# A fused retention and two-layer network: first layer of one group plain, weight sums a group later, seven products from the first group on

## The chip, the cores and the metric

The kernel runs on one core of a Trainium2 chip. The core has five engines with a queue each: TensorE (PE in the profile, its weight loads PEld), VectorE (DVE), ScalarE (ACT), GpSimd (POOL) and SyncE (SP), which here issues the data transfers. An instruction that must wait holds up everything behind it in its own queue. The metric is the device time of one execution in microseconds (us), the median of several runs.

## The reference, cut to what matters

Retention over a sequence, and then a network of two layers on its output `x` (3072 tokens by 512):

```python
state = gamma * state + k_t (outer) v_t          # per batch and head, 64 x 64
y_t   = (1 / sqrt(64)) * q_t @ state
x     = y as (batch * sequence, heads * 64)      # 3072 x 512

h   = x @ w_in                                   # w_in 512 x 2048
g   = h * erf(softplus(h))
out = g @ w_out                                  # w_out 2048 x 512
```

There are 4 batches of 768 positions and 8 heads. All is fp32. The two products with `w_in` and `w_out` are most of the arithmetic.

## The kernel before, in words

Retention is worked off in 24 chunks of 128 tokens, numbered j. The network takes the first 512 tokens in groups 0 to 3 (a group is 512 columns of the first layer), all plainly. The 2560 others are taken 256 tokens at a time, in two groups per 256 tokens: groups 4 to 23. G0 is 4. `s`, the parity of g - G0, says which half of `w_in` and of `w_out` a group uses.

**First layer of a later group.** `hidden_steps` (L951) does not multiply plainly: 26 products of blocks (128 tokens, 128 rows, 256 columns) take the place of 32. They need sums of blocks of `w_in`, formed once per half (`W_SUMS`, 30 entries, `sum_in` at L340), and sums of blocks of `x`, formed once per 256 tokens (`X_SUMS`, 18 entries, `x_sums` at L930). The products go in turn to four PSUM banks ("hp" and "r"). ScalarE copies the first product that belongs to a block of h (L974, L976), and VectorE adds or subtracts each further one (L972), 18 per group. A product can't enter a bank before the earlier one has been read, so VectorE's place in its queue decides when TensorE goes on.

**Gate.** `gate_softplus` and `gate_erf` (ScalarE) and `gated` (VectorE, L854) make g in the tile E of the group.

**Second layer of a later group.** `project_part` (L1027) computes seven products in place of eight, for which `g_sums` (L1009) forms four sums S1 to S4 of E on VectorE and `last_steps` (`sums`, L354) forms four sums T1 to T4 of `w_out` for each half, once. T3 overwrites a block of `w_out`, so that the plain way is open only before it. `put_part` combines the outcome. Before the change the first two later groups, 4 and 5, do it plainly: `project_plain` (L1048), eight parts of four matmul instructions, and `put_plain`. The parts of group g - 1 stand between the steps of group g's first layer, after steps 14, 18 and 24, and after it.

**The order of the work** is written out by hand: the loop over g at the end of the kernel says after which step what is issued, on every engine. In the dictionary `order`, `next_chunk` are five VectorE operations that prepare the next attention chunk, `e_sums` are the S sums, and `last_steps` are the T sums. `sub_begin`, `sub_states` and `sub_visit` are the attention of one chunk, of which `sub_visit(j, g)` stands after the first layer.

**Around group 4.** The 30 sums of `w_in`, half 0, are formed before or in group 4: 16 while the weights are still converted from 64 bits, 4 before the loop, the last 10 between its first ten steps. Those of half 1 follow: 20 on GpSimd (L344) and 10 on VectorE after the layer. The second layer of group 3, 32 matmul instructions of 512 columns (`project`, L901), stands in four parts before, in and after group 4's first layer; then `put_first` copies its four PSUM tiles (L916) and sends them out.

In matmul counts: TensorE does an fp32 matmul as two instructions in the profile, each with its own weight load.

Of the kernel before, what the change touches and what calls it, by code (L numbers as in the profile page):

```python
# [12 lines left out]
F32 = mybir.dt.float32  # L13
# [6 lines left out]
P = 128  # L20
C = 128
TCH = 512
# [114 lines left out]
def kernel(  # L137
# [202 lines left out]
    def sum_in(s, upto, engine=None):  # L340

        assert all(("hidden", 2 * FG + s * FG + u) in done for u in range(FG))
        for to, a, b, sign in W_SUMS[in_sums[s] : upto]:
            (engine or nc.vector).tensor_tensor(  # L344
                w_in_sb[:, s, to], w_in_sb[:, s, a], w_in_sb[:, s, b], op=OP[sign]
            )
        in_sums[s] = max(in_sums[s], upto)
# [12 lines left out]
    def weights():  # L360


        pending = [conversion(n) for n in range(n_p)]
        begun = 0
        for n, steps in enumerate(pending):
            for k, _ in enumerate(steps, start=begun):
                yield
                if n > 4 and n + 1 < n_p and k == 2:
                    next(pending[n + 1])
                    yield  # L370
            begun = int(n > 4)
            if pieces[n] == ("out", 5):
                for k in range(4, 17, 4):
                    sum_in(0, k)
                    yield

    def later_sums():
        for s in range(2):
# [334 lines left out]
    def sub_begin(j, pool=None):  # L713
        SC[j] = [ret_psum(pool) for _ in range(2)]
        sub_scores(j)
        sub_additions(j)

    def sub_visit(j, g):
# [44 lines left out]
        if c:  # L763
            of_state(0)
        last = chunk_of(g - 1)
        if (g - G0) % 2 == 1 and g > G0 + 1:
            clear.update((("o", 0), ("o", 1)))
        new = [
            None if g == G0 else O[last][3][:, 1, :].rearrange("p (u d) -> p u d", d=D),
# [47 lines left out]
    def gate_softplus(g):  # L817


        name = "r" if g < G0 + 2 and g % 2 else "e"  # L820
        E[g] = act.tile([P, N], F32, name=name, bufs=1)
        nc.scalar.activation(E[g], HS[g], AF.Softplus)  # L822

# [85 lines left out]
            done.add(("project", g))  # L909
        pace_around(3.4)  # L910

    def put_first():
        r = act.tile([P, N], F32, name="r", bufs=1)
        for tt in range(TT):
            o = r[:, tt * d_model : (tt + 1) * d_model]
            nc.scalar.copy(o, O[0][tt])  # L916
            nc.sync.dma_start(out[tt * P : (tt + 1) * P, :], o)

    G0 = n_ft // FG
    NG = G0 + (B * S - TCH) // SCH * 2
# [4 lines left out]
    def chunk_of(g):  # L927
        return TCH // SCH + (g - G0) // 2
# [22 lines left out]
    def hidden_steps(g):  # L951

        m, s = chunk_of(g), (g - G0) % 2
        HS[g] = act.tile([P, N], F32, name="h")
        banks = [pool.tile([P, FG, P], F32, name=name) for pool, name in ((ps_h, "hp"), (ps_r, "r")) for _ in range(2)]
        written = set()
        for w, x, bank, first, reads in STEPS:
            to = banks[bank]
            for u in range(2):
                nc.tensor.matmul(  # L960
                    to[:, u, :],
                    w_in_sb[:, s, w, u * P : (u + 1) * P],
                    XS[m](x),
                    start=first and u == 0,
                    stop=True,
                    skip_group_check=True,
                )
            of = to[:, :2].rearrange("p u t -> p (u t)")
            for o, plus in reads:
                h = h_block(g, o)  # L970
                if o in written:
                    nc.vector.tensor_tensor(h, h, of, op=ALU.add if plus else ALU.subtract)  # L972
                elif plus:
                    nc.scalar.copy(h, of)  # L974
                else:
                    nc.scalar.activation(h, of, AF.Copy, scale=-1.0)  # L976
                written.add(o)
            yield

    G = {}  # L980

# [55 lines left out]

    started = set()
    R = {}

    def project_plain(g, i):
        m, s = chunk_of(g), (g - G0) % 2
        t, fh, pair = i // 4, i % 4 // 2, i % 2
        if m not in O:
            O[m] = {i: ps_o.tile([P, 2, DH], F32, name=f"o{i}") for i in (0, 1, 3)}
        for u in range(2 * pair, 2 * pair + 2):
            at = (2 * fh + t) * TCH + u * P
            nc.tensor.matmul(  # L1048
                O[m][t],
                E[g][:, at : at + P],  # L1050
                w_out_sb[:, s, 2 * fh : 2 * fh + 2, u, :],
                start=(s == 0 and i % 4 == 0 and u == 0),
                stop=(s == 1 and i % 4 == 3 and u == 3),
                skip_group_check=True,
            )

    def put_plain(m, t):
        if t == 0:
            R[m] = act.tile([P, 8, DH], F32, name="r", bufs=1)
        r = R[m][:, 2 * t : 2 * t + 2].rearrange("p a c -> p (a c)")  # L1060
        nc.scalar.copy(r, O[m][t].rearrange("p a c -> p (a c)"))
        nc.sync.dma_start(out[m * SCH + t * P : m * SCH + (t + 1) * P, :], r)

    def put_part(m, step):

# [127 lines left out]
    def all_of(steps):  # L1193
        for _ in steps:
            pass

    all_of(weight_steps)

    idle = const.tile([P, 2], F32, name="idle_scalar")
    nc.gpsimd.memset(idle, 1.0)  # L1200

    j = JPC + 2
    gated(G0 - 1)
    all_of(prepared(j))
    load(JPC + 4)
    project(G0 - 1, 0)
    x_sums(G0)
    sub_begin(j)
    sub_states(j)
    sum_in(0, 20)  # L1210

    plain, put = (G0, G0 + 1), None
    for g in range(G0, NG):
        first, even = g == G0, (g - G0) % 2 == 0
        more = j < NJ
        if put is not None and put > chunk_of(G0):
            put_part(put, 0)
        e_sums = iter(()) if g - 1 in plain or first else g_sums(g - 1)
        next(e_sums, None)
        next_chunk = prepared(j + 1) if even or put is None else iter(())  # L1220

        if put is not None:
            order = {18: (e_sums,), 20: (e_sums,), 24: (e_sums, e_sums)}
        else:
            order = {
                10: (next_chunk,), 14: (next_chunk, e_sums), 16: (next_chunk, e_sums),
                18: (next_chunk, e_sums), 20: (e_sums,), 24: (next_chunk,),
            }
        if first:
            order = {n: (next_chunk,) for n in (12, 16, 18, 20, 22)}  # L1230
        elif g == G0 + 2:
            order.update({n: (last_steps,) for n in (12, 15, 20, 22)})
        elif g == G0 + 3:
            order.update({n: (last_steps,) for n in (14, 16)})
        elif g == G0 + 4:
            order.update({n: (last_steps,) for n in (12, 22)})
        for n, _ in enumerate(hidden_steps(g), start=1):
            if first:
                sum_in(0, min(20 + n, len(W_SUMS)))
                if n == 10:  # L1240
                    project(g - 1, 1)
                    nc.gpsimd.tensor_copy(idle[:, :1], w_in_sb[:, 0, W_SUMS[-1][0], :1])
                    sum_in(1, 20, nc.gpsimd)
            if put is not None and n in (14, 16, 18):
                if put > chunk_of(G0):
                    put_part(put, n // 2 - 6)
                elif n < 18:
                    put_plain(put, n // 2 - 7)
            for steps in order.get(n, ()):
                next(steps, None)  # L1250
            if not first and n in (14, 18, 24):
                part = (14, 18, 24).index(n)
                if g - 1 in plain:
                    project_plain(g - 1, part)
                else:
                    project_part(g - 1, (1, 2, 4)[part])
        put = None
        all_of(e_sums)
        all_of(next_chunk)

        nc.scalar.activation(idle[:, 1:], idle[:, 1:], AF.Softplus)
        gate_softplus(g)
        if more:
            sub_visit(j, g)
        if g + 1 < NG and not even:
            x_sums(g + 1)
        if more:
            if even and not first:
                all_of(prepared(j + 2))
            if j + 3 < NJ:  # L1270
                load(j + 3)
            j += 1
        gate_erf(g)
        if first:
            sum_in(1, len(W_SUMS))
            for tt in range(2, TT):
                project(g - 1, tt)
            put_first()
        else:
            if g - 1 in plain:  # L1280
                for part in range(3, 8):
                    project_plain(g - 1, part)
            else:
                for p in (5, 6, 7, 3):
                    project_part(g - 1, p)
            if even:
                put = chunk_of(g - 1)
        if g == NG - 1:
            last_gated(g)
        else:  # L1290
            gated(g)
# [59 lines left out]
```

## Time and profile before

The median is 672.5 us (three runs, 672.39 to 672.66). The profiled execution has a span of 670.3 us.

| engine | busy us | share of the span | instructions |
|---|---|---|---|
| TensorE, matmul | 658.7 | 98% | 6192 |
| TensorE, weight loads | 547.4 | 82% | 6192 |
| VectorE | 510.6 | 76% | 1095 |
| ScalarE | 272.8 | 41% | 395 |
| GpSimd | 22.1 | 3% | 42 |

| operation | instructions | mean ns of one |
|---|---|---|
| first layer, product of 128 columns (L960) | 2080 | 275 |
| second layer, seven products, 256 columns (L1027) | 1000 | 379 to 382 |
| second layer, plain, 512 columns (L1048) | 64 | 596 |
| VectorE, product into h (L972) | 360 | 416 to 419 |
| VectorE, sum of `w_out` blocks (L354) | 8 | 1218 |
| VectorE, S sum (L1009) | 68 | 677 to 685 |
| VectorE, sum of `w_in` blocks (L344) | 40 | 427 |
| GpSimd, sum of `w_in` blocks (L344) | 20 | 782 |

How to read it: matmuls overlap in the array, so the mean duration of one is longer than the time from one start to the next, and a busy TensorE is not one at its peak. Where an engine's idle time is given with a releaser ("<-DVE h L972"), that is the instruction whose end let it go on.

### The profile page before, as it was taken

To read this page: it belongs to the slowest core of one execution; us is meant where nothing else is said; L and a number is where in the kernel's file an instruction comes from. 1 tells how busy PE (TensorE), PEld (TensorE's weight loads), DVE (VectorE), ACT (ScalarE), POOL (GpSimd) and SP (SyncE) were. 2 spreads that over 40 slices of the span, in tenths; PEclk is the share of its full clock that TensorE was granted. 3 is DMA by queue.
4 is the path that set the end of the run, shared out by engine and by line. 5 is a ranking of instruction groups with operands and counts; after the bars stand their busy time and mean duration, and the time that the engine had idled before them with its cause. 6 is when DMAs were issued, how large, how long until landed. Compare 5 with 4: busy or idle time off the path is not lost.

```text
span 670.3 us, 15241 instructions
## 1 busy us (share of the span) xinstructions
PE 658.7 (98%) x6192; PEld 547.4 (82%) x6192; DVE 510.6 (76%) x1095; ACT 272.8 (41%) x395; POOL 22.1 (3%) x42
## 2 busy tenths in 40 slices
PE   8999999989999999999999999999999999999998
PEld 7744444466766998999999999999999999999997
DVE  5999999986778679678678787787687688476464
ACT  3467453425333344243343442442542542533440
POOL 1000000253000000000000000000000000000000
PEclk9999999999999999999999999999999999999999
DMA  9999744333321222322222221231232220000000
GB/s 188 227 253 240 196 138 97 62 61 62 105 45 29 68 42 45 69 45 47 60 51 46 47 65 36 46 80 35 45 78 38 42 55 1 2 32 1 1 33 31
DMA packets 156725, 47.68 MB, mean 71 GB/s; under 512 B 143088, under 2 KB 147568, under 8 KB 156656
## 3 DMA queue, kind: packets, MB, share of 16 engines
q1 hardware_dynamic: 156240, 46.72, 31.8%
q8 instruction: 48, 0.79, 0.5%
q14 instruction: 21, 0.17, 0.1%
q10 hardware_dynamic: 416, 0.01, 0.0%
HBM read 40.39 MB, written 6.29 MB: 70 GB/s over the span
## 4 chain that ended last, share of the span: by engine, by line
PE 77%; DVE 9%; SPq 5%; issue 3%; DMA 3%; ACT 2%; DVEq 0%; ACTq 0%
PE o L1027 33%; PE hp L960 22%; PE r L960 11%; SPq L187 4%; PE o L1048 4%; DMA kq<-in_k_dram 2%; PE r L741 2%; PE hp L633 1%; DVE w_out_sb L317 1%; PE o L901 1%; DVE w_out_sb L325 1%; PE o L777 1%; DVE xs L325 1%; DVE h L972 1%; DVE w_in_sb L331 1%
## 5 line engine op out<-in xcount | busy, mean ns | idle before, releaser
L960 PE MATMUL hp<-xs,w_in_sb 128*128 128x128 f32 x1040 | 146.3, 276 | 4.7 <-DVE h L972 3.8
L960 PEld LDWEIGHTS hp<-xs,w_in_sb 128*128 128x128 f32 x1040 | 134.6, 192 | 12.3 <-DVE h L972 7.2
L972 DVE TENSOR_TENSOR h<-h,hp 128x256 f32<-128x256 f32 x200 | 81.9, 419 | 77.9 <-PE hp L960 73.4
L1027 PE MATMUL o<-w_out_sb,h 128*128 128x256 f32 (+1 forms) x584 | 129.5, 379 | 0.4 <-DVE r L1306 0.4
L1027 PEld LDWEIGHTS o<-w_out_sb,h 128*128 128x128 f32 x584 | 108.6, 190 | 15.4 <-DVE r L1306 0.6
L1027 PE MATMUL o<-w_out_sb,e 128*128 128x256 f32 x432 | 102.2, 379 | 0.0
L822 ACT ACTIVATE e<-h 128x2048 f32<-128x2048 f32 x21 | 40.1, 1911 | 123.0 <-DVE h L972 123.0
L1027 PEld LDWEIGHTS o<-w_out_sb,e 128*128 128x128 f32 x432 | 78.2, 191 | 8.5
L972 DVE TENSOR_TENSOR h<-h,r 128x256 f32<-128x256 f32 x160 | 60.1, 416 | 25.1 <-PE r L960 23.7
L974 ACT COPY h<-hp 128x256 f32<-128x256 f32 x40 | 14.9, 373 | 153.1 <-PE hp L960 124.9
L960 PE MATMUL r<-xs,w_in_sb 128*128 128x128 f32 x480 | 66.7, 275 | 0.8 <-DVE am L640 0.8
L960 PEld LDWEIGHTS r<-xs,w_in_sb 128*128 128x128 f32 x480 | 60.1, 192 | 1.4 <-PE hp L960 0.9
L865 PE MATMUL hp<-xT,w_in_sb 128*128 128x512 f32 (+2 forms) x144 | 56.5, 548 | 0.0
L854 DVE TENSOR_TENSOR e<-h,e 128x1024 f32<-128x1024 f32 x40 | 46.9, 1214 | 8.1 <-ACT e L835 8.1
L960 PE MATMUL hp<-xT,w_in_sb 128*128 128x128 f32 x320 | 48.9, 275 | 0.0
L865 PEld LDWEIGHTS hp<-xT,w_in_sb 128*128 128x128 f32 x144 | 25.8, 190 | 27.0 <-issue 24.6
L960 PEld LDWEIGHTS hp<-xT,w_in_sb 128*128 128x128 f32 x320 | 43.6, 192 | 2.3 <-issue 1.4
L835 ACT ACTIVATE e<-e 128x2048 f32<-128x2048 f32 (+1 forms) x22 | 40.2, 1833 | 0.2
L976 ACT ACTIVATE h<-hp 128x256 f32<-128x256 f32 x60 | 23.0, 384 | 32.1 <-PE hp L960 30.7
L960 PE MATMUL r<-xT,w_in_sb 128*128 128x128 f32 x240 | 33.3, 275 | 0.0
L835 ACT ACT_TABLE_LOAD x24 | 30.8, 1283 | 0.4
L960 PEld LDWEIGHTS r<-xT,w_in_sb 128*128 128x128 f32 x240 | 30.0, 192 | 0.0
(161 smaller groups left out, 811.6 us busy)
## 6 DMA issues: line engine op xcount, KB each, us to landing
w_out_sb<-in_moe_w_out_dram SPq DMA_DIRECT2D x14, 512.0 KB, 5.6
kq<-in_k_dram SPq DMA_DIRECT2D x23, 256.0 KB, 4.0
v<-in_v_dram SPq DMA_DIRECT2D x23, 256.0 KB, 3.2
out_dram<-r SPq DMA_DIRECT2D x23, 256.0 KB, 2.7
kq<-in_q_dram SPq DMA_DIRECT2D x288, 16.0 KB, 1.8
kb<-in_k_dram SPq DMA_DIRECT2D x288, 16.0 KB, 1.7
w_in_sb<-in_moe_w_in_dram SPq DMA_DIRECT2D x8, 512.0 KB, 11.1
w_in_sb<-in_moe_w_in_dram SPq DMA_DIRECT2D x8, 256.0 KB, 8.8
```

Of the source, the lines that this page charges most:

```text
L187: nc.sync.dma_start(to[part, u * C : (u + 1) * C].rearrange("p (a d) -> p a d", d=32), src[2 * u + s, :, d * 32 : (d + 1) * 32].rearrange( ...
L325: nc.vector.scalar_tensor_tensor(power, hi, 1 << 31, power, op0=ALU.bitwise_and, op1=ALU.bitwise_or)
L822: nc.scalar.activation(E[g], HS[g], AF.Softplus)
L835: nc.scalar.activation(E[g][:, half], E[g][:, half], AF.Erf)
L854: nc.vector.tensor_tensor(E[g][:, half], HS[g][:, half], E[g][:, half], op=ALU.mult)
L865: nc.tensor.matmul(HP_[ft][:, t], w_in_of(ft, kk), XC[0][:, kk, t], start=(kk == 0), stop=(kk == n_k - 1),)
L960: nc.tensor.matmul(to[:, u, :], w_in_sb[:, s, w, u * P : (u + 1) * P], XS[m](x), start=first and u == 0, stop=True, skip_group_check=True,)
L972: nc.vector.tensor_tensor(h, h, of, op=ALU.add if plus else ALU.subtract)
L974: nc.scalar.copy(h, of)
L976: nc.scalar.activation(h, of, AF.Copy, scale=-1.0)
L1027: nc.tensor.matmul(O[m][i][:, half, at], G[g][a][:, u * P : (u + 1) * P], w_out_sb[:, s, OUT[b], u, at], start=i not in started, stop=(s = ...
L1048: nc.tensor.matmul(O[m][t], E[g][:, at : at + P], w_out_sb[:, s, 2 * fh : 2 * fh + 2, u, :], start=(s == 0 and i % 4 == 0 and u == 0), sto ...
```

## The change: what it does and what it is for

Group 4's first layer is computed plainly, by the new `hidden_plain`: eight tiles of four matmuls with 256 columns, each copied by ScalarE. It needs no sums of `w_in`. So the sums of half 0 move from ahead of group 4 to after it (10 on VectorE, 20 on GpSimd), where group 6 is the first to need them, and those of half 1 go all to VectorE, during and after group 4's first layer. The second layer of groups 4 and 5 is done with seven products as that of all others is: `project_plain` and `put_plain` go, the T sums of half 0 move to group 5 and those of half 1 to group 6, and the S sums of groups 4 and 5 are added. The second layer of group 3 stands behind group 4's first layer as a whole, and `put_first` sends each of its tiles out as soon as it is done, by way of the places in group 3's gate tile that the tile's matmuls have read. The aim is to let TensorE start group 4 without waiting for sums, and to spare an eighth of two groups' second layer.

```diff
-            if pieces[n] == ("out", 5):
-                for k in range(4, 17, 4):
-                    sum_in(0, k)
-                    yield
...
-        name = "r" if g < G0 + 2 and g % 2 else "e"
+        name = "r" if g < 4 and g % 2 else "e"
...
+    def put_first(tt):
+        o = E[G0 - 1].rearrange("p (u t c) -> p t u c", u=FG, t=TT)[:, tt]
+        nc.scalar.copy(o, O[0][tt].rearrange("p (u c) -> p u c", u=FG))
...
+    def hidden_plain(g):
...
+        for f, u in itertools.product(range(2), range(FG)):
+            to = ps_h.tile([P, TCH], F32, name="hp")[:, :SCH]
+            for kk in range(n_k):
+                nc.tensor.matmul(
+                    to, w_in_of((2 * f + s) * FG + u, kk), x[:, kk], start=kk == 0, stop=kk == n_k - 1
+                )
+            nc.scalar.copy(h[:, f, u], to.rearrange("p (t c) -> p t c", t=2))
+            yield
...
-    load(JPC + 4)
-    project(G0 - 1, 0)
-    x_sums(G0)
-    sub_begin(j)
-    sub_states(j)
-    sum_in(0, 20)
+    load(j + 2)
+    for n, _ in enumerate(hidden_plain(G0), start=1):
+        if n == 3:
+            sub_begin(j)
+    x_sums(G0)
+    sub_states(j)
+    all_of(prepared(j + 1))
+    sum_in(1, 20)
+    project(G0 - 1, 0)
+    nc.scalar.activation(idle, idle, AF.Softplus)
+    gate_softplus(G0)
+    sub_visit(j, G0)
+    load(j + 3)
+    put_first(0)
+    gate_erf(G0)
+    sum_in(1, len(W_SUMS))
+    for tt in range(1, TT):
+        project(G0 - 1, tt)
+        put_first(tt)
+    gated(G0)
+    sum_in(0, 10)
+    sum_in(0, len(W_SUMS), nc.gpsimd)
...
+        if g <= G0 + 2:
+            order = {
+                10: (next_chunk,), 12: (last_steps,), 14: (next_chunk, e_sums), 16: (last_steps,),
+                18: (next_chunk, e_sums), 20: (last_steps,), 22: (next_chunk,), 24: (next_chunk, e_sums),
+            }
...
+        if g <= G0 + 2:
+            next(last_steps)
...
-            if g - 1 in plain:
-                for part in range(3, 8):
-                    project_plain(g - 1, part)
-            else:
-                for p in (5, 6, 7, 3):
-                    project_part(g - 1, p)
+        for p in (5, 6, 7, 3):
+            project_part(g - 1, p)
```

More of the change, by code (lines that the diff above doesn't have):

```diff
@@ L765, in sub_visit @@
         last = chunk_of(g - 1)
-        if (g - G0) % 2 == 1 and g > G0 + 1:
+        if (g - G0) % 2 == 1:
             clear.update((("o", 0), ("o", 1)))
@@ L910, in project @@
         pace_around(3.4)
[L912 to L917, printed above, removed]
+    def put_first(tt):
+        o = E[G0 - 1].rearrange("p (u t c) -> p t u c", u=FG, t=TT)[:, tt]
+        nc.scalar.copy(o, O[0][tt].rearrange("p (u c) -> p u c", u=FG))
+        nc.sync.dma_start(out[tt * P : (tt + 1) * P, :].rearrange("p (u c) -> p u c", u=FG), o)
     G0 = n_ft // FG
@@ L978, in hidden_steps @@
             yield
+    def hidden_plain(g):
+        m, s = chunk_of(g), (g - G0) % 2
+        HS[g] = act.tile([P, N], F32, name="h")
+        h = HS[g].rearrange("p (f t u c) -> p f u t c", f=2, t=2, u=FG)
+        x = XC[m // 2][:, :, m % 2 * SCH : (m % 2 + 1) * SCH]
+        for f, u in itertools.product(range(2), range(FG)):
[6 more added lines that the diff above has]
+            yield
+        done.update(("hidden", (2 * f + s) * FG + u) for f in range(2) for u in range(FG))
     G = {}
@@ L1039 @@
     R = {}
[L1041 to L1062, printed above, removed]
     def put_part(m, step):
@@ L1197 @@
     all_of(weight_steps)
-    idle = const.tile([P, 2], F32, name="idle_scalar")
+    idle = const.tile([P, 1], F32, name="idle_scalar")
     nc.gpsimd.memset(idle, 1.0)
@@ L1204 @@
     all_of(prepared(j))
-    load(JPC + 4)
-    project(G0 - 1, 0)
-    x_sums(G0)
-    sub_begin(j)
-    sub_states(j)
-    sum_in(0, 20)
-    plain, put = (G0, G0 + 1), None
-    for g in range(G0, NG):
-        first, even = g == G0, (g - G0) % 2 == 0
+    load(j + 2)
[6 more added lines that the diff above has]
+    sum_in(1, 20)
+    project(G0 - 1, 0)
+    nc.scalar.activation(idle, idle, AF.Softplus)
[11 more added lines that the diff above has]
+    sum_in(0, len(W_SUMS), nc.gpsimd)
+    j += 1
+    put = None
+    for g in range(G0 + 1, NG):
+        even = (g - G0) % 2 == 0
         more = j < NJ
-        if put is not None and put > chunk_of(G0):
+        if put is not None:
             put_part(put, 0)
-        e_sums = iter(()) if g - 1 in plain or first else g_sums(g - 1)
-        next(e_sums, None)
+        e_sums = g_sums(g - 1)
+        next(e_sums)
         next_chunk = prepared(j + 1) if even or put is None else iter(())
@@ L1228 @@
             }
[L1229 to L1236, printed above, removed]
-        for n, _ in enumerate(hidden_steps(g), start=1):
[L1238 to L1243, printed above, removed]
+        if g <= G0 + 2:
[3 more added lines that the diff above has]
+            }
+        for n, _ in enumerate(hidden_steps(g), start=1):
             if put is not None and n in (14, 16, 18):
[L1245 to L1248, printed above, removed]
+                put_part(put, n // 2 - 6)
             for steps in order.get(n, ()):
                 next(steps, None)
-            if not first and n in (14, 18, 24):
-                part = (14, 18, 24).index(n)
-                if g - 1 in plain:
-                    project_plain(g - 1, part)
-                else:
-                    project_part(g - 1, (1, 2, 4)[part])
+            if n in (14, 18, 24):
+                project_part(g - 1, {14: 1, 18: 2, 24: 4}[n])
         put = None
@@ L1259 @@
         all_of(next_chunk)
-        nc.scalar.activation(idle[:, 1:], idle[:, 1:], AF.Softplus)
+        nc.scalar.activation(idle, idle, AF.Softplus)
         gate_softplus(g)
@@ L1267 @@
         if more:
-            if even and not first:
+            if even:
                 all_of(prepared(j + 2))
@@ L1273 @@
         gate_erf(g)
[L1274 to L1280, printed above, removed]
-                for part in range(3, 8):
-                    project_plain(g - 1, part)
-            else:
-                for p in (5, 6, 7, 3):
-                    project_part(g - 1, p)
-            if even:
-                put = chunk_of(g - 1)
+        for p in (5, 6, 7, 3):
+            project_part(g - 1, p)
+        if even:
+            put = chunk_of(g - 1)
         if g == NG - 1:
```

## The prediction, made before the changed kernel ran

> **What bounds the kernel now.** I read the page first: the engines' busy shares and the 40 slices. TensorE is busy nearly everywhere and its granted clock is full throughout, so a saving counts only where it shortens TensorE's own row.
>
> ```profile
> PE 658.7 (98%) x6192; PEld 547.4 (82%) x6192; DVE 510.6 (76%) x1095; ACT 272.8 (41%) x395; POOL 22.1 (3%) x42
> PEld 7744444466766998999999999999999999999997
> PEclk9999999999999999999999999999999999999999
> ```
>
> The weight loads say more than the matmuls: in the ninth to thirteenth slice (134 to 218 us) they stand at 6 and 7 tenths, and at 8 and 9 from then on. The change touches that stretch. So next I cut the trace into stages, each from the first matmul of one group's first layer to that of the next (columns: stage length, then busy us and instructions of each engine).
>
> ```profile
> 127.42:161.58 34.16, 29.90 (x281) 20.79 (x280) 28.05 (x76) 10.19 (x16) 15.33 (x21) 1.00 0.33 61
> 161.58:190.11 28.53, 27.80 (x265) 19.81 (x264) 19.73 (x51) 11.80 (x19) 0.00 (x0) 1.00 0.31 77
> 190.11:218.58 28.47, 28.10 (x265) 19.56 (x264) 21.51 (x40) 10.14 (x15) 0.00 (x0) 1.00 0.20 37
> 218.58:244.50 25.92, 25.92 (x289) 24.29 (x288) 18.87 (x50) 11.10 (x17) 0.00 (x0) 1.00 0.27 61
> 244.50:270.85 26.35, 26.26 (x289) 24.13 (x288) 22.53 (x43) 10.39 (x16) 0.00 (x0) 1.00 0.22 41
> 270.85:296.76 25.91, 25.91 (x273) 24.29 (x272) 18.87 (x51) 10.13 (x15) 0.00 (x0) 1.00 0.28 63
> ```
>
> The first row is group 4 with the rest of group 3's second layer, the others are groups 5 to 9. A stage without a stall is 25.9 us. Groups 5 and 6 take 2.6 us more each, and group 4's row has unused TensorE time. The waits of TensorE from 127 to 300 us tell which engine ends it:
>
> ```profile
> PE hp L960 <- DVE h L972: 3.8, 5, 1.4
> PE r L960 <- DVE am L640: 0.8, 1, 0.8
> PE hp L960 <- ACT h L974: 0.7, 1, 0.7
> ```
>
> VectorE empties the PSUM banks too late. The last view is VectorE and GpSimd while GpSimd forms weight sums (140.7 to 156.4 us):
>
> ```profile
> L551 DVE TENSOR_TENSOR kq<-kq,kq_b 128x512 f32<-128x512 f32 x1 | 1.1, 1131 | 0.0
> L542 DVE TENSOR_TENSOR kq<-kq,kq_s 128x512 f32<-128x512 f32 x1 | 0.8, 781 | 0.0
> L344 POOL TENSOR_TENSOR w_in_sb<-w_in_sb x20: 718/727/1187, 140.7 to 155.8; 128x256 f32<-128x256 f32 x20
> ```
>
> The same two VectorE operations last 681 and 686 ns one stage later; GpSimd's sums run from 718 to 1187 ns.
>
> **What the Trainium skill says.** "SBUF — State Buffer", section "Who interferes with whom": a VectorE instruction with two SBUF inputs contends with a GpSimd instruction that reads SBUF; one with a single SBUF input does not. The trace agrees: +450 and +95 ns on the two rows above, a weight sum at 675 instead of 420 ns, one multiplication unharmed; the bank additions, which have one input in PSUM, keep 0.41 us. "TensorE: Matmul & The Clock Gate", section "Back-to-back issue gap": the spacing of matmuls does not fall in proportion to their columns, since weight loads share the pipeline. Here, too, though the page's figures are not those of this fp32 stream: pieces of the chain give 0.89 us for 8 matmul instructions of 128 columns (0.111 each), 1.73 us for 8 of 256 (0.216), 1.72 us for 4 of 512 (0.43). "Perfetto Trace Analysis", section "Tensor Engine Instruction (MATMUL, LD_WEIGHTS)": matmul ends are modelled, and VectorE, ScalarE and GpSimd are strict FIFOs. So I count starts, not busy time, and count what stands ahead in a queue; the 1.27 us hole at 145.2 us, in which TensorE waits for an addition queued behind a chunk's multiplication of 0.78 us, agrees.
>
> **The change part by part.**
>
> *Group 4's first layer plainly.* Removed: 104 instructions of 128 columns, 104 x 0.1115 = 11.6 us. Added: 8 tiles x 4 matmuls, 64 instructions of 256 columns, 8 x 1.73 = 13.9 us. TensorE's work grows by 2.3 us. In return the layer no longer waits for weight sums or bank additions: the tiles are complete in PSUM and ScalarE copies each (373 ns for a 128x256 copy) while TensorE makes the next (1.73 us). The old stretch from 127.42 to 161.58 holds group 3's second layer 13.9 (32 x 0.434), scores and updates 1.1 (130.95 to 132.04), first layer 11.6, attention visit 1.8 (152.83 to 154.61): 28.4 of 34.16, so 5.8 us of stall. The new one holds 13.9 + 13.9 + 1.1 + 1.8 = 30.7. I see no stall there. The scores come third among the tiles, at about 132.6, when VectorE has long prepared them (at 129 in the old run, and it sheds 6.2 us of sums at 106.9). The 20 sums of the other half, 20 x 0.39 = 8 us, lie beside TensorE and end near 146, and the next chunk, whose last load is issued at 133.4 and lands 1.7 us later, is ready by 139 for the visit at 146; the last ten (4.4 us) end near 154; gating, 2.4 us, and ten sums of the first half, about 4 us, end near 160.5. Group 5's first layer starts near 158.1 and its first VectorE addition is due at 160.4. Gain 34.16 - 30.7 = 3.5 us. Included: the four output copies, which at 161.78 to 163.83 all stood ahead of group 5's bank copies (0.7 us of stall), are spread out, and only the last, 0.6 us, remains; TensorE can fill four banks (1.8 us) meanwhile.
>
> *Seven products for groups 4 and 5.* Plain: 32 instructions of 512, 32 x 0.434 = 13.9 us. Seven: 56 of 256, 56 x 0.22 = 12.3. TensorE's stage becomes 11.6 + 12.3 + 2.0 (visit) = 25.9, as in the 25.92 row, against 28.53 and 28.47.
>
> *What VectorE gets for it.* In stages 5 and 6, beside 18 additions (6.5 us at about 0.36 from start to start) and five operations of the next attention chunk (3.1), come three w_out sums (3 x 1.15 = 3.5) and three of the four S sums (3 x 0.6 = 1.8) within the first layer: 14.9 us, in the 16.8 us that first layer and three products last; a fourth S sum and a fourth w_out sum follow. The old stage 6 had 14.2 there (6.5 + 3.1 + 4 x 1.15) and lost 1.0 us (28.47 against 27.5 of work). Queued: step 24's addition stands behind chunk work and sums, and step 25 writes the same bank. Then the fourth S sum stands ahead of the attention state's addition, for which the visit's last matmuls wait. For stage 6 I take 0.5 + 0.3 = 0.8 us of stall.
>
> *Twenty sums on GpSimd during stage 5.* They begin when VectorE's ten end (160.5) and take 20 x 0.73 = 14.6 us undisturbed. Meanwhile VectorE has ten operations with two SBUF inputs (three multiplications, three w_out sums, four S sums). What each loses is unknown: from 0 to a whole GpSimd operation, 0.73. The four samples above (0.45, 0.10, 0.26, 0) have a mean of 0.2, which I take: 2 us, on a VectorE that had hardly 2 us spare. Stepping through the 26 steps with 0.2 added, step 24's addition is done 17.55 us after the stage's start, where TensorE wanted it at 16.0; TensorE ends the layer 1.75 us late, and the state's addition costs 0.7 more. Stage 5: 25.9 + 2.5 = 28.4. Bounds: 26.7 at zero, about 30 at half an operation each (10 x 0.37, less 0.1 spare). GpSimd, delayed as often, ends near 180; group 6 wants the sums from 186 on. Hidden, with 5 us to spare.
>
> *Small things.* Later stages lose the two w_out sums of group 8, whose row is 26.35 against 25.91: 0.4. Loads: the queue still issues one chunk in 17 us and needs one per 26; nothing waits. The output goes out through group 3's gate buffer; nobody wants that buffer before group 7. Zero for both.
>
> Sum: 3.5 + (28.53 - 28.4 = 0.1) + (28.47 - 26.7 = 1.8) + 0.4 = 5.8 us. 672.5 - 5.8 = 666.7.
>
> **The rivals.** (A) No collisions that matter: stage 5 like stage 6, 1.7 us better, 665.0. For it: one sample of four lost nothing, and TensorE had slack at products 14 and 18. Against: VectorE's queue is full in just this stage. (B) VectorE becomes the bound of stages 5 and 6: the sums bunched after steps 14 to 16 meet GpSimd each time, stage 5 takes 30.5 and stage 6 27.7, 3.1 us worse, 669.8. For it: three of four samples collided. Against: old stage 6, almost as full, lost only 1.0. (C) Slower: GpSimd and VectorE lock each other out, and each of the ten operations waits for a whole GpSimd operation, 7.3 us. Then stage 5 is 25.9 + 7.3 + 0.7, and about 1 more since the sums of x for group 6 come late behind all that: 34.9, 6.4 worse than before; with 3.5, 1.0 (stage 6 at 27.5) and 0.4 gained, 674.0. For it: a FIFO passes every delay on. Against: no sample lost more than 0.45, and GpSimd itself would still be done near 186.
>
> **How the numbers follow.** Forecast 0.6, A 0.2, B 0.13, C 0.07. The range 664.3 to 669.6 takes in A and the half-operation bound. Faster than 671.2: forecast, A and B less a little: 0.91; same 0.03; slower 0.06.
>
> **What would show it.** Right: group 5's first layer starting near 158, no waits of TensorE from 127 to 158; stage 5 near 28.4 with waits on VectorE's additions and two-input operations above 0.75 us; stage 6 near 26.7; group 8 at 25.9; everything after shifted unchanged. Wrong: a hole before group 5, GpSimd ending past 186 with a wait for it, or stages 5 and 6 both over 28.

## The result, and the profile after

The changed kernel takes 668.4 us (median of four runs, 667.4 to 669.5) against 672.6: ratio 0.9936, 95% interval 0.9915 to 0.9957, 4.1 us faster. It was forecast faster by 5.8 us, at 666.7. Measured a second time (six runs), it took 668.9, ratio 0.9940 (0.9924 to 0.9956).

The page: weight loads are 84% busy instead of 82%. The ninth to thirteenth slice, at 6, 6, 7, 6 and 6 tenths before, now stand at 7, 6, 7, 9 and 9.

```profile
PE 657.5 (99%) x6200; PEld 557.1 (84%) x6200; DVE 512.4 (77%) x1089; ACT 272.5 (41%) x394; POOL 22.9 (3%) x41
PEld 7744454576799999999999999999999999999997
```

The stages are cut as before, from one group's first matmul to the next group's (length, then busy us of each engine). The first row is group 4 with what is left of group 3's second layer, then come groups 5 to 9.

```profile
127.53:158.33 30.80, 30.80 (x241) 20.80 (x240) 24.69 (x65) 11.73 (x19) 0.00 (x0) 1.00 0.35 64
158.33:187.93 29.60, 27.09 (x290) 24.35 (x289) 25.63 (x56) 10.63 (x16) 18.16 (x19) 1.00 0.35 77
187.93:214.44 26.51, 26.42 (x290) 24.20 (x289) 24.43 (x47) 10.40 (x16) 0.00 (x0) 1.00 0.21 39
214.44:240.37 25.93, 25.93 (x290) 24.29 (x289) 20.57 (x54) 10.14 (x15) 0.00 (x0) 1.00 0.29 64
240.37:266.30 25.93, 25.93 (x290) 24.29 (x289) 20.52 (x41) 10.40 (x16) 0.00 (x0) 1.00 0.23 43
266.30:292.20 25.90, 25.90 (x274) 24.26 (x273) 18.88 (x51) 10.14 (x15) 0.00 (x0) 1.00 0.28 62
```

Group 4's row is free of stalls, 3.4 us shorter than 34.16. Stage 6 is 2.0 us shorter, group 8's 0.4. Stage 5 is 1.1 us longer than the 28.53 it was, though TensorE has 1.6 us less to do in it (13.9 - 12.3). The sum is 4.7 us; the two spans differ by 4.6 (670.3 and 665.7), since group 4 starts 0.1 us later. From group 9 on the kernels are alike.

TensorE's waits between 127 and 300 us; all lie in stage 5:

```profile
PE hp L952 <- DVE h L964: 2.2, 3, 1.3
PE o L1035 <- DVE w_out_sb L354: 0.3, 1, 0.3
```

They come to 2.5 us, and stage 5 is 3.1 longer than stage 6. The other 0.6 is in TensorE's busy time, 27.09 us against 26.42. As an estimate, each hole breaks the overlap of matmuls that last 0.275 us and start 0.111 apart, and four times the difference is 0.66: a hole costs somewhat more than its idle time.

What held VectorE up is seen in its groups while GpSimd forms the sums (159.4 to 178.1 us; line, operation, count, then busy us and mean ns of one):

```profile
L354 DVE TENSOR_TENSOR w_out_sb<-w_out_sb 128x1024 f32<-128x1024 f32 x3 | 4.2, 1387 | 0.0
L964 DVE TENSOR_TENSOR h<-h,hp 128x256 f32<-128x256 f32 x8 | 3.1, 406 | 1.6 <-PE hp L952 1.5
L547 DVE TENSOR_TENSOR kb<-kb,kq_b 128x512 f32<-128x512 f32 x1 | 1.2, 1236 | 0.0
L547 DVE TENSOR_TENSOR kq<-kq,kq_b 128x512 f32<-128x512 f32 x1 | 1.2, 1236 | 0.0
L538 DVE TENSOR_TENSOR kq<-kq,kq_s 128x512 f32<-128x512 f32 x1 | 1.1, 1051 | 0.0
```

GpSimd's own row, over the whole run (shortest, median and longest ns; one of the twenty sums runs early, at 118.7 us, the other nineteen from 159.4 on):

```profile
L344 POOL TENSOR_TENSOR w_in_sb<-w_in_sb x20: 720/732/1721, 118.7 to 177.3; 128x256 f32<-128x256 f32 x20
```

The multiplications of the next chunk last 1.05 to 1.24 us, and 0.68 one stage later; the bank additions (L964), with one input in PSUM, keep 0.41. GpSimd's sums, 732 ns as a rule, take up to 1721. How that reaches TensorE is seen in VectorE's queue, in order of time (start, length):

```profile
171.43 0.41 DVE L964 TENSOR_TENSOR h<-h,r 128x256 f32<-128x256 f32 x1
171.76 1.24 DVE L547 TENSOR_TENSOR kq<-kq,kq_b 128x512 f32<-128x512 f32 x1
172.92 1.21 DVE L1017 TENSOR_TENSOR h<-h,e 128x512 f32<-128x512 f32 x1
174.05 0.74 DVE L964 TENSOR_TENSOR h<-h,hp 128x256 f32<-128x256 f32 x2
```

TensorE at the same time, with its idle time and what ended it in brackets:

```profile
174.51 1.16 PE L952 MATMUL hp<-xs,w_in_sb 128*128 128x128 f32 x8 [1.35 <-DVE h L964]
```

A multiplication and an S sum, each lengthened by about 0.55, stand ahead of the two bank additions. TensorE goes on as soon as the first of these is done (174.46 us).

The runs of the changed kernel lie in two clumps, and that can't be understood without the clock: of ten runs, five at 667.4 to 668.1 us have a mean granted clock of 0.999 or 1.000, five at 669.2 to 671.2 have 0.997. The median of 668.4 lies between the clumps. A trace of the second kind was taken with the repetition. Its stage 5, and then the three stretches of 3.41 us around the fall of the clock (the clock is the figure after the five engines, ahead of the last two):

```profile
158.72:189.95 31.23, 28.71 (x289) 25.64 (x288) 25.84 (x56) 10.62 (x16) 18.15 (x19) 0.95 0.33 72
173.54:176.96 3.42, 1.76 (x12) 1.50 (x12) 3.42 (x7) 0.00 (x0) 3.34 (x4) 1.00 1.14 318
176.96:180.37 3.41, 3.41 (x12) 2.88 (x11) 2.14 (x5) 0.00 (x0) 1.37 (x2) 0.50 0.18 52
180.37:183.78 3.41, 3.41 (x137) 3.15 (x137) 2.53 (x6) 1.67 (x1) 0.00 (x0) 1.00 0.19 42
```

The clock is full to 176.96 us, just after the last of stage 5's holes, half for 3.41 us, and full again. Half the clock for 3.41 us is 1.7 us of work lost, and stage 5 is 1.6 us longer than in the other trace, 31.23 against 29.60.

### The profile page after: what moved, and what is told of

Its sections match the earlier page's. It is cut to its first block, busy times and chain, and to the rows that moved or that the text cites. A ratio compares the mean times of both kernels' runs of the same rounds, so it can differ in the third digit from the quotient of the medians.

```text
span 665.7 us, 15224 instructions
## 1 busy us (share of the span) xinstructions
PE 657.5 (99%) x6200; PEld 557.1 (84%) x6200; DVE 512.4 (77%) x1089; ACT 272.5 (41%) x394; POOL 22.9 (3%) x41
## 4 chain that ended last, share of the span: by engine, by line
PE 72%; SPq 10%; DVE 9%; issue 4%; DMA 2%; ACT 2%; DVEq 0%; ACTq 0%
PE o L1035 35%; PE hp L952 20%; PE r L952 10%; SPq L187 9%; DMA kq<-in_k_dram 2%; PE r L737 1%; DVE w_out_sb L317 1%; PE hp L629 1%; DVE w_out_sb L325 1%; PE o L773 1%; DVE xs L325 1%; DVE w_in_sb L331 1%; DVE w_out_sb L322 1%; DVE w_out_sb L313 1%; DVE xs L313 1%
## 5 line engine op out<-in xcount | busy, mean ns | idle before, releaser
L1035 PE MATMUL o<-w_out_sb,h 128*128 128x256 f32 (+1 forms) x648 | 144.0, 380 | 0.4 <-DVE r L1284 0.4
L952 PE MATMUL hp<-xs,w_in_sb 128*128 128x128 f32 x988 | 138.7, 275 | 2.3 <-DVE h L964 2.2
L1035 PEld LDWEIGHTS o<-w_out_sb,h 128*128 128x128 f32 x648 | 120.4, 190 | 17.5 <-DVE r L1284 0.6
L952 PEld LDWEIGHTS hp<-xs,w_in_sb 128*128 128x128 f32 x988 | 128.3, 192 | 6.3 <-DVE h L964 3.5
L964 DVE TENSOR_TENSOR h<-h,hp 128x256 f32<-128x256 f32 x190 | 77.5, 417 | 66.7 <-PE hp L952 62.0
L1035 PE MATMUL o<-w_out_sb,e 128*128 128x256 f32 x480 | 113.7, 380 | 0.3 <-DVE w_out_sb L354 0.3
L1035 PEld LDWEIGHTS o<-w_out_sb,e 128*128 128x128 f32 x480 | 86.8, 190 | 10.0 <-DVE w_out_sb L354 0.5
L964 DVE TENSOR_TENSOR h<-h,r 128x256 f32<-128x256 f32 x152 | 56.9, 415 | 22.3 <-PE r L952 21.2
L952 PE MATMUL r<-xs,w_in_sb 128*128 128x128 f32 x456 | 63.3, 275 | 0.0
L952 PEld LDWEIGHTS r<-xs,w_in_sb 128*128 128x128 f32 x456 | 57.0, 192 | 0.0
L968 ACT ACTIVATE h<-hp 128x256 f32<-128x256 f32 x57 | 21.9, 384 | 29.6 <-PE hp L952 28.3
```

The source lines that it names most:

```text
L952: nc.tensor.matmul(to[:, u, :], w_in_sb[:, s, w, u * P : (u + 1) * P], XS[m](x), start=first and u == 0, stop=True, skip_group_check=True,)
L1035: nc.tensor.matmul(O[m][i][:, half, at], G[g][a][:, u * P : (u + 1) * P], w_out_sb[:, s, OUT[b], u, at], start=i not in started, stop=(s = ...
```

## The experiments

The theory after the result: the sums on GpSimd lengthen VectorE's operations with two SBUF inputs, VectorE then falls behind in the one stage in which it has no slack, and TensorE waits. The rivals: the T and S sums overload VectorE by themselves; or one of the two halves of the change (plain first layer, seven products) isn't worth what was counted.

**All sums on VectorE** (e1_vector_sums).

```diff
+    sum_in(1, 10)
     gated(G0 - 1)
...
     x_sums(G0)
+    sum_in(1, 19)
     sub_states(j)
     all_of(prepared(j + 1))
-    sum_in(1, 20)
+    sum_in(1, len(W_SUMS))
+    sum_in(0, 8)
...
     gate_erf(G0)
-    sum_in(1, len(W_SUMS))
+    sum_in(0, 18)
...
     gated(G0)
-    sum_in(0, 10)
-    sum_in(0, len(W_SUMS), nc.gpsimd)
+    sum_in(0, len(W_SUMS))
```

> All sixty sums of w_in blocks on VectorE: ten of half 1 ahead of group 3's gating, nine more before the attention states, the rest and then those of half 0 after the next chunk; GpSimd has none. Collision theory (VectorE's operations with two SBUF inputs wait for GpSimd's): stage 5 falls from 29.6 to about 26.5 us, as stage 6 (26.5); group 5 still starts near 158.3; total 3.1 us below the changed kernel's 668.4, about 665.3. Rival (the T and S sums alone overload VectorE in stage 5): stage 5 stays near 29.6, no change. Second rival (VectorE has no room for twenty more sums before group 5): group 5 starts late by up to 4 us and the gain is gone, 668 or more.

Measured: 664.5 us (664.2 to 664.8), ratio to the kernel before 0.9878 (0.9864 to 0.9891). Groups 5 and 6:

```profile
158.20:184.72 26.52, 26.43 (x289) 24.19 (x288) 22.86 (x57) 10.62 (x16) 0.00 (x0) 1.00 0.39 86
184.72:211.24 26.52, 26.43 (x290) 24.20 (x289) 24.44 (x47) 10.39 (x16) 0.00 (x0) 1.00 0.21 40
```

Stage 5 equals stage 6. The T sums, with the order of work that goes with them, cost each of the two stages 0.6 us (26.52 against the 25.9 of later stages, which have S sums but no T sums). Both rivals of the expectation fall. Group 5 starts no later: VectorE had idled 4.0 us ahead of group 3's gating and 3.5 ahead of the attention states, which the sums of half 1 now fill. All four runs had the full clock and lie within 0.6 us: of the 3.9 us to the changed kernel's median, 3.1 are stage 5 and about 0.7 the clock. This version beats both kernels.

**Writes only** (e2_memsets, e5_memsets_long). GpSimd's twenty sums are left out; instead it fills the blocks with zeros, in the first kernel once each, in the second three times each, after a first fill that starts as VectorE's ten sums end (159.3 us). The edit of the second:

```diff
-    sum_in(0, len(W_SUMS), nc.gpsimd)
+    nc.gpsimd.memset(w_in_sb[:, 0, 9], 0.0)
+    for to, *_ in W_SUMS[10:] * 3:
+        nc.gpsimd.memset(w_in_sb[:, 0, to], 0.0)
```

> As the changed kernel, but GpSimd's twenty sums of half 0 are left out, and GpSimd fills the same twenty blocks with zeros instead, which only writes. Collision of reads: no VectorE operation of stage 5 is lengthened, stage 5 about 26.5 us, about 665.3 in all. If any GpSimd traffic collides: two-input operations still lose some 0.4 us each and stage 5 stays above 28. Rival (VectorE's own load): stage 5 stays near 29.6.

Measured 664.9 (664.6 to 666.1). It decides less than was meant: a fill took only 0.28 us, and the ten that fell into stage 5's time were over in 2.8. That the time is lost with the sums is shown, the kind of traffic is not. Hence the long form:

> The changed kernel with GpSimd's twenty sums of half 0 left out; instead GpSimd fills blocks of the same half with zeros sixty-one times, from the end of VectorE's ten sums on, so that it writes through all of stage 5's first layer (the earlier run with zeros was over after 2.8 us). If only GpSimd's reads hold VectorE up: two-input operations keep 0.68 us, stage 5 26.5, about 664.9. If writing collides as well: two-input operations above 0.8 us, stage 5 above 28, 666.5 or more.

Measured 664.4 (664.2 to 664.5). The row of stage 5, and GpSimd, which writes through most of it, in order of time:

```profile
158.16:184.68 26.52, 26.43 (x290) 24.20 (x288) 22.57 (x56) 10.63 (x16) 15.60 (x61) 1.00 0.39 86
159.51 15.69 POOL L1213 MEMSET w_in_sb<- 128x256 f32 x60
```

VectorE's groups in the same stretch:

```profile
L547 DVE TENSOR_TENSOR kb<-kb,kq_b 128x512 f32<-128x512 f32 x1 | 0.7, 685 | 0.0
L538 DVE TENSOR_TENSOR kq<-kq,kq_s 128x512 f32<-128x512 f32 x1 | 0.7, 684 | 0.0
```

Not one VectorE operation is longer for it. GpSimd's reads collide, its writes don't.

**One read** (e6_copies). The sums are left out again, and forty copies of a block stand in their place.

```diff
-    sum_in(0, len(W_SUMS), nc.gpsimd)
+    nc.gpsimd.memset(w_in_sb[:, 0, 9], 0.0)
+    for to, x, *_ in W_SUMS[10:] * 2:
+        nc.gpsimd.tensor_copy(w_in_sb[:, 0, to], w_in_sb[:, 0, x])
```

> The changed kernel with the twenty sums left out and forty GpSimd copies of a block in their place, which read one block and write one. If reading is what collides: two-input operations of VectorE lengthen as with the sums, by up to the length of one copy, and stage 5 is above 27.5, about 666 or more; if it takes two read operands on GpSimd: stage 5 26.5, about 664.9.

Measured 666.4 (666.2 to 666.6). The row of stage 5, and the copies, in order of time:

```profile
158.50:186.88 28.38, 27.12 (x289) 24.36 (x288) 24.40 (x56) 10.63 (x16) 20.48 (x41) 1.00 0.36 80
159.86 20.59 POOL L1213 COPY w_in_sb<-w_in_sb 128x256 f32<-128x256 f32 x40
```

VectorE's groups while they run:

```profile
L354 DVE TENSOR_TENSOR w_out_sb<-w_out_sb 128x1024 f32<-128x1024 f32 x3 | 4.3, 1439 | 0.0
L1017 DVE TENSOR_TENSOR h<-h,e 128x512 f32<-128x512 f32 x1 | 0.9, 878 | 0.0
L538 DVE TENSOR_TENSOR kq<-kq,kq_s 128x512 f32<-128x512 f32 x1 | 0.8, 805 | 0.0
```

One operand is enough. Stage 5 is 26.5 us with fills or nothing, 28.4 with copies (0.40 us each where nothing delays them) and 29.6 with sums (0.73). The ten VectorE operations with two SBUF inputs that meet the copies lose 0.19 us each on average, about half a copy. Sums are longer than copies and also read a second operand; these runs do not separate the two.

**Seven products alone** (e3_seven_only). The kernel before, in which groups 4 and 5 have seven products; the order of T and S sums is that of the changed kernel.

```diff
-    plain, put = (G0, G0 + 1), None
+    put = None
...
-        e_sums = iter(()) if g - 1 in plain or first else g_sums(g - 1)
+        e_sums = iter(()) if first else g_sums(g - 1)
...
+        elif g <= G0 + 2:
+            order = {
+                10: (next_chunk,), 12: (last_steps,), 14: (next_chunk, e_sums), 16: (last_steps,),
+                18: (next_chunk, e_sums), 20: (last_steps,), 22: (next_chunk,), 24: (next_chunk, e_sums),
+            }
```

> The kernel before with the seven products for groups 4 and 5 alone; group 4's first layer keeps its 26 products and GpSimd its sums of half 1 during it. My account: the start of group 5 stays near 161.6; stage 5 about 26.6 and stage 6 26.5 instead of 28.5 each, group 8 25.9 instead of 26.35: 4.3 us faster, about 668.2. Rival (moving the T and S sums into stages 5 and 6 costs what the products spare): stages of 28 or more, 672.

Measured 669.3 (669.2 to 669.6), ratio 0.9950 (0.9937 to 0.9962): 3.3 us faster, 1.1 less than expected. Stage 6 is 26.51 as expected, stage 5 27.72 and not 26.6. TensorE waits twice in stage 5:

```profile
PE hp L960 <- ACT h L974: 0.7, 1, 0.7
PE hp L960 <- DVE h L972: 0.3, 1, 0.3
```

The second is a late bank addition. The first, which the kernel before has too and which I had left out of the sum, is the four output copies ahead of group 5's bank copies on ScalarE. The changed kernel spreads them out, and has no such wait. (The prediction counts this gain under group 4; the wait lies in stage 5's row.)

**The plain first layer alone** (e4_first_only). The changed kernel with `project_plain` and `put_plain` back for groups 4 and 5, and the T sums in groups 6 to 8 as before. GpSimd's sums stay in stage 5.

```diff
-    put = None
+    plain, put = (G0, G0 + 1), None
...
-        e_sums = g_sums(g - 1)
-        next(e_sums)
+        e_sums = iter(()) if g - 1 in plain else g_sums(g - 1)
+        next(e_sums, None)
...
-        for p in (5, 6, 7, 3):
-            project_part(g - 1, p)
+        if g - 1 in plain:
+            for part in range(3, 8):
+                project_plain(g - 1, part)
+        else:
+            for p in (5, 6, 7, 3):
+                project_part(g - 1, p)
```

> The changed kernel with the second layers of groups 4 and 5 plain again, and the T sums where they were before. My account: group 5 starts near 158.3, 3.25 us earlier; stage 5 27.5 (no stall: with no T and S sums in it VectorE has room for the collisions, though they are there), stage 6 28.5, group 8 26.35: 4.3 us faster, about 668.2. Rival (GpSimd's sums cost TensorE their 3.1 us whatever else VectorE has): stage 5 30 or more and 671.

Measured 668.3 (667.9 to 670.0), ratio 0.9938 (0.9925 to 0.9950): 4.3 us faster, as expected. The row of stage 5:

```profile
158.30:185.86 27.56, 27.56 (x265) 19.73 (x264) 19.05 (x51) 10.62 (x16) 14.54 (x19) 1.00 0.38 84
```

VectorE's groups in it, beside GpSimd's sums:

```profile
L547 DVE TENSOR_TENSOR kq<-kq,kq_b 128x512 f32<-128x512 f32 x1 | 1.2, 1214 | 0.0
L538 DVE TENSOR_TENSOR kq<-kq,kq_s 128x512 f32<-128x512 f32 x1 | 1.1, 1061 | 0.0
```

Operations collide here too, and TensorE has no wait in the stage: VectorE is 19 us busy in it and not 25.6. The rival, that the sums on GpSimd cost TensorE their 3.1 us in any case, falls. It takes both: collisions and a VectorE without slack.

**The changed kernel again** (after_again), unchanged, beside the runs with fills and copies.

> The changed kernel as it is, on the same chip and beside the same runs of the kernel before as the two others. Expected: 667.5 to 669.5 as in the first runs, stage 5 29.6.

Measured 668.9 (667.6 to 671.2; the slowest lies outside the expected range). Its trace is the one with the fallen clock, stage 5 31.23, not the 29.6 expected.

The parts: the first layer alone gives 4.3 us, seven products alone 3.3, together 7.6. The change gives 4.1, and with the sums on VectorE 8.0 (672.58 - 664.54). So 3.4 to 3.9 us of the two parts' worth were lost where they met.

## Why the prediction was right, and where it was off

*Group 4's row* was forecast at 30.7 without a stall and is 30.80 without one. The plain layer takes TensorE 14.0 us (127.53 to 132.80 and 133.89 to 142.62), forecast 13.9, and the ten VectorE sums ended at 159.3, forecast 160.5. The next chunk's load held VectorE up, 1.7 us to 137.3, and no matmul waited for it. *Seven products*: stage 6 was forecast at 26.7 and is 26.5. *Small things*: group 8 gained the 0.4, the output copies did not stall group 5.

*Stage 5* is the term that was mis-sized: "Stage 5: 25.9 + 2.5 = 28.4". The mechanism was the right one, as "SBUF — State Buffer", section "Who interferes with whom", states it, the fills and copies included. (The page excepts VectorE's two-port modes, which the prediction passes over. The transposes here, with one SBUF input, kept their 0.69 us.) The size came from four samples with a mean of 0.2 us per operation. Eight VectorE operations with two SBUF inputs met GpSimd (two of the ten came after it was done) and, measured against stage 6, lost 0.37, 0, 0.56, 0.53, 0.53, 0.56, 0.53 and 0: 3.1 us, 0.38 each, which I had named as the half-operation bound (0.37). The bound's stage of "about 30" is what was measured, 29.6. Why four samples were too few is seen in the traces: the two engines take turns, as the last section shows. In stage 5 a multiplication, an S sum and a T sum follow each other, GpSimd gets its turn after each, and the next waits for it; in the stretch of the samples such operations stood singly. GpSimd lost as well: its nineteen sums took 18.6 us and not 19 x 0.73 = 13.9. They ended at 178.0, ten us ahead of group 6, so the tail of rival C never came near.

*Not foreseen*: the clock. I took it as full "throughout" and read it only in the kernel before. Half the runs have a lower mean clock, and the one such trace loses another 1.6 us in stage 5 to it. Of the 1.7 us between 5.8 forecast and 4.1 measured, 1.2 is the size of the collisions (29.6 for 28.4) and 0.7 the clock (the median of 668.44 against 667.72 of the first trace's run); stage 6 gave 0.2 back.

*A misreading that cost nothing*: the prediction says of the spacing of matmuls that it is out of proportion to their columns "Here, too". Its own figures, 0.111, 0.216 and 0.43 us for 128, 256 and 512 columns, are in proportion to within 4%. The sums used these measured spacings, so nothing in them changes.

Rival A, "No collisions that matter", was put at 665.0; the kernels without GpSimd's reads take 664.4 to 664.9. Rival B's total, 669.8, is a little nearer to the 668.4 measured than the forecast is (1.4 and 1.7 us). What tells them apart is where the time went: B put a loss into both stages, 30.5 and 27.7 us, and stage 6, in which GpSimd is idle, takes 26.5.

## What to carry to other kernels

Work moved to GpSimd isn't free for VectorE, even where no one waits for it: count the VectorE operations with two SBUF inputs beside it, and price each at half a GpSimd operation (0.38 us of 0.73 with sums, 0.19 of 0.40 with copies), or at up to three quarters where such operations follow each other (0.53 to 0.56 of 0.73), not at a mean from a stretch where they stand singly. Look first for idle time in VectorE's own queue ahead of the busy stage; here twenty more sums fitted there and GpSimd wasn't needed. Two savings that are each real can spend the same slack: check what the sum of them leaves on the engine that feeds the bound.

## What the runs showed of the hardware

**Turns.** In these traces a VectorE operation with two SBUF inputs and a GpSimd sum take turns: the one that starts while the other is under way waits for it. Two pairs of the changed kernel, first a T sum that starts 0.11 us ahead of a GpSimd sum, then a multiplication that starts 0.04 us after one:

```profile
165.34 1.21 DVE L354 TENSOR_TENSOR w_out_sb<-w_out_sb 128x1024 f32<-128x1024 f32 x1
165.45 1.69 POOL L344 TENSOR_TENSOR w_in_sb<-w_in_sb 128x256 f32<-128x256 f32 x1
167.10 0.72 POOL L344 TENSOR_TENSOR w_in_sb<-w_in_sb 128x256 f32<-128x256 f32 x1
167.14 1.24 DVE L547 TENSOR_TENSOR kb<-kb,kq_b 128x512 f32<-128x512 f32 x1
```

The T sum has its 1.21 us and the GpSimd sum takes 1.69 instead of 0.73; then the GpSimd sum has 0.72 and the multiplication takes 1.24 instead of 0.68. The eight operations of stage 5 all follow this: the two T sums that lost nothing started 0.11 and 0.07 us ahead of a GpSimd sum, and the six others started while one was under way. The four samples of the kernel before fit too: the multiplication that lost nothing started 0.07 us ahead of a GpSimd sum, the three others during one.

**The clock.** In the repetition's trace holes of 0.47, 0.40, 1.35 and 0.31 us, 2.5 in all, within 167 to 176.4 us, are followed by 3.41 us at half clock; in the first trace, with holes of the same sizes, the clock stays full. "TensorE: Matmul & The Clock Gate", section "What's actually happening", describes a free-running window of 3413 ns of activity and a clock of either full or half. The two traces agree with that: the low stretch has the window's length, and whether it comes changes from run to run. The section "A second HAM failure mode: psum-queue depth-cycling" tells of another kernel in which frequent short idles between groups of matmuls make the clock swing; the holes here are short too, the longest 1.35 us.

That these holes brought the clock down is argued, not shown. For it: it fell right after them, and all 26 runs of the other six kernels, which have fewer holes in stage 5 or none, are at 0.999 or 1.000. The kernel before has holes of 1.27 and 1.36 us in group 4, and its clock never fell in the 20 runs beside the experiments. But they lie further apart. Its 3.41 us with the most idle time, beside the stretch of the first trace that corresponds to the one ahead of the fall (the full-clock record of that trace ends at 664.70 us; this is counted back from there in steps of 3.413):

```profile
149.05:152.46 3.41, 1.88 (x15) 1.69 (x15) 2.64 (x7) 0.00 (x0) 3.41 (x6) 1.00 0.22 35
173.18:176.59 3.41, 1.77 (x11) 1.53 (x12) 3.41 (x7) 0.00 (x0) 3.33 (x4) 1.00 1.11 307
```

TensorE is busy 1.88 us in the kernel before, 1.77 in the trace that kept the clock and 1.76 in the one that lost it. So what kept the clock in one of two nearly equal stretches stays open; where the window's bounds fall among the holes doesn't tell these two traces apart.
